# First scores ahead of the last Mish block, and an output product cut at the attention outputs

## The chip, the cores and the metric

The kernel runs on one core of a Trainium2 chip. That core has a matrix engine (TensorE, PE in the profile; PEld are its weight loads), a vector engine (VectorE, DVE), an activation engine (ScalarE, ACT), a general engine (GpSimd, POOL) and a queue that issues DMAs (SyncE, SP). The engines run side by side. Each works through its own list of instructions in order, and they meet only through semaphores. The metric is the device time in microseconds (us) of one launch; lower is better. Three runs of the kernel before took 481.72, 482.39 and 482.79 us.

## What is computed

Attention with a softmax whose denominator has one extra term, over 8 batches of 12 heads, 448 rows, head size 64. Its output, seen as 3584 rows of 768, goes through a layer of 2048 with the Mish function:

```python
scores = scale * np.matmul(q, k.transpose(0, 1, 3, 2))
m = np.max(scores, axis=-1, keepdims=True)
e = np.exp(scores - m)
attn = e / (np.sum(e, axis=-1, keepdims=True) + np.exp(-m) + 1e-09)
x = (attn @ v).transpose(0, 2, 1, 3).reshape(3584, 768)
h = x @ w_in
g = h * np.tanh(np.log1p(np.exp(h)))     # Mish
out = g @ w_out
```

## The kernel before

**Units.** Two heads make a pair, three pairs make a unit, and two units hold one batch. Unit u works on the scores and exponentials of its own three pairs, on the attention outputs of unit u-1, on half of the first layer (x @ w_in, eight blocks of 128 features) for batch (u-2)//2, and on parts of the output product (g @ w_out) of earlier batches. Units 2 to 15 have scores; units 4 to 15 are "grouped": the order of work in their twelve steps is written out by hand in the table `GROUPED` (L484). That table has one list for even and one for odd units. Units 16 to 19 finish the layer. The program has a manual schedule: instructions stand on each engine in the order in which the Python code emits them.

**Names used from here on.** All are of one grouped unit.

- S0, S1, S2, S4, ... are score steps of two matmuls (L247 and L250, 64 rows of the array each, side by side); R3, R7 and R11 are the fourth step of each pair, one full matmul (L255). Steps 0-3 belong to the first pair, 4-7 to the second, 8-11 to the third.
- r0 to r11 are the maxima of these steps on DVE (L269), e0 to e11 their exponentials on ACT (L282). A step S has two exponentials, a step R one. Step s of a pair uses PSUM tile sc0, sc1 or sc2; step R uses mo1.
- A0, A1, A2 are the attention outputs of the pairs of the unit before (eight matmuls, L354). They go to mo1 (in odd units the third goes to sc0) and X0, X1, X2 take them out on DVE (L363).
- A *fill* is two matmuls of the output product (L443); a *part* is eight fills for 128 rows and either a half (384) or a quarter (192) of the columns. A part takes its PSUM tile, mo0, with its first fill. DVE empties it after the last (evacuation E, L430), and only then can the next part begin: mo1 is kept out of the free list in grouped units.
- M0 to M7 are the blocks of the first layer (six matmuls, L377, then one Mish on ACT, L383). They use sc0, mo0, mo1, sc0, mo0, mo1, mo0, mo1 (`MISH_BANK`, L514). T1, T3 and T5, after M1, M3 and M5, turn q and k of the next unit on PE (L189); DVE takes out q (L208), ACT takes out k (L218).
- D0, D1, D2 are the DMAs that turn the exponentials for the attention output (L321, tile eT). They follow the denominators (L295, L299) and the normalisation (L317 on DVE for two pairs, L315 on POOL for the third), which need all exponentials of the unit. They sit in SP's queue with the loads of q, k, v (L128) and the stores (L408).

**Order of a unit.** Twelve steps: step n emits its exponentials e(n), flushes the evacuations that are due (`flush_late`), and then what the table lists: fills ("fill", count), scores ("sc", steps), an attention output ("av", pair). Behind the twelve steps come M0 to M7 with T1, T3, T5 and the normalisation between them, and after M7 the scores S0, S1, S2 of the next unit (L680). Last stands a small exponential (L689) that loads the exponential's table on ACT. The other switch of tables comes with the first Mish.

The table of even units before, with the three scores in front: `S0 S1 S2 | 6 fills, A0 | 2 fills, R3 S4 S5 | 4 fills | S6, A1 | 2 | 2, R7 S8 S9 | 4 | 4, S10, A2 | 3 | 2, R11 | 3 | M0...`. Odd units start with 5 and 3 fills ahead of `R3 S4 S5`, have A0 where even units have A1, A1 where those have A2, and A2 behind R11.

`plan` (L463) gives each unit its parts, 32 fills in all (24 in unit 4). The rows of the plan list (group, row block, first quarter, number of quarters).

Of the kernel before, what the change touches and what calls it, by code (L numbers as in the profile page):

```python
# [19 lines left out]
def kernel(  # L20
# [24 lines left out]
    FF_U = FF_T // UNITS_PER_B  # L45
    NH = d_model // 2
    SCALE = 1.0 / float(D) ** 0.5
    N_PAIRS = B * HP
    STEPS = 4
# [3 lines left out]
    def pool(name, bufs, space=None):  # L53
# [18 lines left out]
    sc_tiles = [  # L72
        psum.tile([128, 2, 512], FP32, tag=f"sc{i}", name=f"sc{i}") for i in range(3)
    ]
    mo_tiles = [psum.tile([128, 512], FP32, tag=f"mo{i}", name=f"mo{i}") for i in range(2)]
# [32 lines left out]
    def flush_late():  # L108
        while late:
            late.popleft()()  # L110
# [40 lines left out]
    def load_w(n):  # L151
        for _ in range(min(n, len(pieces))):
            dst, src = pieces.popleft()
            nc.gpsimd.dma_start(out=dst, in_=src.rearrange("(a p) c -> p a c", p=128))
# [301 lines left out]
    first_mm2 = 2 * UNITS_PER_B  # L456
# [6 lines left out]
    plan = {}  # L463
    for g in range(B // 2):
        u0 = first_mm2 + 4 * g
        if g == 0:
            plan[u0] = [(0, 0, 0, 2), (0, 1, 0, 2), (0, 2, 0, 1)]
            plan[u0 + 1] = [(0, 0, 2, 2), (0, 1, 2, 2), (0, 2, 1, 1), (0, 2, 2, 2)]
        else:
            plan[u0] = plan.pop(u0) + [(g, 0, 0, 2), (g, 1, 0, 1), (g, 0, 2, 2)]  # L470
            plan[u0 + 1] = [(g, 1, 2, 2), (g, 2, 0, 2), (g, 1, 1, 1), (g, 2, 2, 2)]
        plan[u0 + 2] = [(g, 4, 0, 2), (g, 4, 2, 2), (g, 5, 0, 1), (g, 5, 1, 2)]
        plan[u0 + 3] = [(g, 3, 0, 2), (g, 3, 2, 2), (g, 5, 3, 1), (g, 6, 0, 2)]
        if g < B // 2 - 1:
            plan[u0 + 4] = [(g, 6, 2, 2)]
        else:
            plan[u0 + 3] += [(g, 6, 2, 1), (g, 6, 3, 1)]
# [4 lines left out]


    GROUPED = (  # L484
        (
            [("fill", 6), ("av", 0)],
            [("fill", 2), ("sc", (3, 4, 5))],
            [("fill", 4)],
            [("sc", (6,)), ("av", 1)],
            [("fill", 2)],  # L490
            [("fill", 2), ("sc", (7, 8, 9))],
            [("fill", 4)],
            [("fill", 4), ("sc", (10,)), ("av", 2)],
            [("fill", 3)],
            [("fill", 2), ("sc", (11,))],
            [("fill", 3)],
            [],
        ),
        (
            [("fill", 5)],  # L500
            [("fill", 3), ("sc", (3, 4, 5))],
            [("fill", 4)],
            [("sc", (6,)), ("av", 0)],
            [("fill", 2)],
            [("fill", 2), ("sc", (7, 8, 9))],
            [("fill", 4)],
            [("fill", 4), ("sc", (10,)), ("av", 1)],
            [("fill", 3)],
            [("fill", 2), ("sc", (11,))],
            [("fill", 1), ("av0", 2)],  # L510
            [("fill", 2)],
        ),
    )
    MISH_BANK = (0, 1, 2, 0, 1, 2, 1, 2)  # L514
    to_gather = deque()

# [63 lines left out]
    for u in range(UNITS_PER_B, N_UNITS + 2 * UNITS_PER_B):  # L580
        attn = u < N_UNITS
        filler = deque()
        for part in plan.get(u, []):
            filler.extend(mm2_part(*part))
        total, done, acc = sum(w for _, w in filler), 0, 0.0
        p0 = u * UNIT_PAIRS
        grouped = attn and p0 >= GROUP_FROM
        if u == N_UNITS:
            mo_free.append(mo_tiles[1])
        end = min((u + 1) * UNIT_PAIRS, N_PAIRS) * STEPS  # L590

        for n in range(steps):
            pi, s = divmod(n, STEPS)
            p, idx = p0 + pi, p0 * STEPS + n
            late_tp = u == UNITS_PER_B and n == STEPS
            if late_tp:
                transpose_pair(p0 + 2)
            exps(idx)
            if grouped:
                flush_late()  # L600
                for what, arg in GROUPED[u % 2][n]:
                    if what == "fill":
                        for _ in range(min(arg, len(filler))):
                            fn, w = filler.popleft()
                            fn()
                            done += w
                    elif what in ("av", "av0"):
                        bank = mo_tiles[1] if what == "av" else sc_tiles[0][:, 0, :]
                        av_pair(p0 - UNIT_PAIRS + arg, bank=bank)
                    else:  # L610
                        flush_late()
                        for i in arg:
                            scores(p0 * STEPS + i)
                if n in LOAD_AT:
                    load_pair(p0 + LOAD_AT.index(n) + LEAD)
                    cast_pair(p0 + LOAD_AT.index(n) + LEAD - 1)
                if u - UNITS_PER_B < len(W_AT):
                    load_w(W_AT[u - UNITS_PER_B].get(n, 0))
                continue
            if late_tp:  # L620
                evac_qk(p0 + 2)
            if u == UNITS_PER_B + 1:
                for part in TURN_AT[1].get(n, []):
                    turn_on_pe(*part)
            flush_late()
            acc += weight[n]
            want = int(total * acc / sum(weight) + 1e-6)
            while done < want:
                fn, w = filler.popleft()
                fn()  # L630
                done += w
            scores_ahead(end)
            if n in LOAD_AT:
                load_pair(p0 + LOAD_AT.index(n) + LEAD)
                cast_pair(p0 + LOAD_AT.index(n) + LEAD - 1)
            if u - UNITS_PER_B < len(AV_AT):
                early = AV_AT[u - UNITS_PER_B]
                if n in early:
                    av_pair(early[n])
                if u == UNITS_PER_B:  # L640
                    for part in TURN_AT[0].get(n, []):
                        turn_on_pe(*part)
            elif u == N_UNITS and n in LAST_AV_AT:
                av_pair(p0 - UNIT_PAIRS + LAST_AV_AT.index(n))
            if u - UNITS_PER_B < len(W_AT):
                load_w(W_AT[u - UNITS_PER_B].get(n, 0))
        assert done == total

        moe = u < N_UNITS + UNITS_PER_B
        b, w = (u - UNITS_PER_B) // UNITS_PER_B, u % UNITS_PER_B  # L650
        nxt = p0 + UNIT_PAIRS
        todo = sorted(range(p0, nxt), key=lambda p: p in BY_PE)
        to_group = attn and nxt >= GROUP_FROM
        if to_group and nxt == GROUP_FROM:
            flush_late()
            mo_free.remove(mo_tiles[1])
            rg["next"] = N_PAIRS * STEPS
        for f in range(FF_U):
            if moe:
                bank = sc_tiles[0][:, 0, :] if f == 1 else None  # L660
                if to_group:
                    bank = (sc_tiles[0][:, 0, :], None, mo_tiles[1])[MISH_BANK[f]]
                mm1_mish(b, w * FF_U + f, bank)
                if f == 6 and to_gather:
                    gather_mid(to_gather.popleft())
            if u == UNITS_PER_B and f in (2, 6):
                load_w(1)
            if not attn:
                continue
            if f == 0:  # L670
                denominators(att[p0]["whole"])
                normalise(todo[0], dma=todo[0] not in BY_PE)
            if f in (1, 3, 5):
                transpose_pair(nxt + f // 2, bank=f // 2 % 2)
                evac_qk(nxt + f // 2)
            if not to_group and f in (4, 6):
                scores_ahead(nxt * STEPS + f // 2 - 1)
            if f == FF_U - 1 and not to_group:
                scores_ahead(nxt * STEPS + 3)
            if f == FF_U - 1 and to_group and nxt < N_PAIRS:  # L680
                for s in range(3):
                    scores(nxt * STEPS + s)
            if f == 3:
                normalise(todo[1], dma=todo[1] not in BY_PE)
            if f == 4:
                normalise(todo[2], dma=todo[2] not in BY_PE, on_pool=True)
        if attn and u + 1 < N_UNITS:

            nc.scalar.activation(out=one, in_=zero, func=AF.Exp)  # L689
        if moe and w == UNITS_PER_B - 1:  # L690
            to_gather.append(b)
            if u == N_UNITS + UNITS_PER_B - 1:
                gather_mid(to_gather.popleft())
# [32 lines left out]
```

## Time and profile before

| what | value |
|---|---|
| median of three runs | 482.39 us |
| the profiled execution, its own time | 483.19 us |
| its span, first to last instruction | 481.1 us |
| mean granted TensorE clock | 0.982 |
| PE busy | 439.6 us, 91% |
| ACT busy | 348.7 us, 72% |
| DVE busy | 328.9 us, 68% |
| POOL busy | 193.9 us, 40% |
| chain that ended last, by engine | PE 72%, DVE 14%, ACT 6%, issue 4%, DMA 3% |

The profiled execution takes 2.09 us more than its span: that is what lies around the first and the last instruction. "Busy" of PE counts the modelled end of each matmul and so overlaps a little; where a matmul starts is the safer thing to read. An entry such as `[0.74 <-DVE negm L269]` at the end of a row of the timeline says how long the engine was idle before that row and whose instruction ended last before it went on.

### The profile page before, as it was taken

The page shows a single profiled execution, that of the slowest core. Times are in us where ns is not written, and L with a number is a line of the kernel's source. Part 1 is how long each engine was busy: PE and PEld are TensorE (multiplying, and loading weights), DVE is VectorE, ACT ScalarE, POOL GpSimd, SP SyncE. Part 2 cuts the span into 40 slices and gives each one's busy share as a digit, 9 for nine tenths or more (in the row PEclk, how much of TensorE's full clock was granted, in tenths as well). Part 3 has the DMA queues.
Part 4 walks back from the last instruction along what each step waited for, and adds up shares of the span by engine and source line. Part 5 has one row for each costly group of instructions (what it writes and reads, how often), then busy time and mean ns, then how long its engine had stood idle before and what let it go on. Part 6 is the DMA issues. An engine that isn't in the chain of part 4 may idle for free.

```text
span 481.1 us, 8897 instructions
## 1 busy us (share of the span) xinstructions
PE 439.6 (91%) x3064; PEld 237.6 (49%) x3064; DVE 328.9 (68%) x652; ACT 348.7 (72%) x919; POOL 193.9 (40%) x365
## 2 busy tenths in 40 slices
PE   4565887998899899999999999999999999999997
PEld 2233544544455454545455554545454545556565
DVE  4888987878786868777785968587777868330021
ACT  5979678879796879788887979697977979302300
POOL 4877809255616244253636344343535340300000
PEclk9998698999999999999999999999999999999999
DMA  8999959999999989898999999898999594860213
GB/s 220 226 240 205 239 99 234 160 197 244 188 217 266 215 225 216 224 194 235 206 241 173 252 156 245 185 223 210 203 228 201 153 180 117 143 153 1 67 33 100
DMA packets 202381, 90.37 MB, mean 188 GB/s; under 512 B 159072, under 2 KB 198880, under 8 KB 202336
## 3 DMA queue, kind: packets, MB, share of 16 engines
q1 hardware_dynamic: 194848, 83.51, 80.0%
q0 software_dynamic: 7488, 6.29, 8.5%
q8 instruction: 24, 0.39, 0.3%
q14 instruction: 21, 0.17, 0.1%
HBM read 45.61 MB, written 11.01 MB: 118 GB/s over the span
## 4 chain that ended last, share of the span: by engine, by line
PE 72%; DVE 14%; ACT 6%; issue 4%; DMA 3%; POOL 0%; DVEq 0%; SPq 0%; ACTq 0%; POOLq 0%
PE mo L443 26%; PE mo L377 21%; DVE negm L269 9%; PE sc L377 7%; PE sc L247 5%; PE mo L354 5%; ACT en L282 4%; PE sc L189 3%; DMA eT<-en 2%; DVE o_sb L430 2%; PE mo L332 2%; PE mo L255 1%; DVE en L317 1%; PE sc L354 1%; DMA k_f<-in_k_dram 1%
## 5 line engine op out<-in xcount | busy, mean ns | idle before, releaser
L282 ACT ACTIVATE en<-sc,negm 128x448 bf16<-128x448 f32 x300 | 186.6, 645 | 12.8 <-DVE negm L269 8.9
L269 DVE TENSOR_REDUCE negm<-sc 128x2 f32<-128x896 f32 (+1 forms) x156 | 158.0, 1048 | 37.9 <-PE sc L250 30.7
L443 PE MATMUL mo<-w_out_sb,gT 128*128 128x384 bf16 (+1 forms) x912 | 138.6, 301 | 1.5
L377 PE MATMUL mo<-xT,w_in_sb 128*128 128x448 bf16 x594 | 122.4, 352 | 0.6 <-DVE xT L363 0.6
L443 PEld LDWEIGHTS <-gT 128*128 128x128 bf16 x912 | 81.0, 98 | 58.5 <-issue 23.2
L383 ACT ACTIVATE gT<-mo 128x448 bf16<-128x448 f32 x99 | 53.9, 545 | 72.7 <-PE mo L377 72.7
L377 PEld LDWEIGHTS <-w_in_sb 128*128 128x128 bf16 x768 | 72.8, 98 | 66.5 <-issue 5.3
L315 POOL TENSOR_SCALAR en<-en,rden 128x448 bf16<-128x448 bf16 x122 | 77.7, 654 | 58.1 <-DVE rden L307 54.2
L430 DVE COPY o_sb<-mo 128x384 f32<-128x384 f32 (+1 forms) x65 | 32.5, 500 | 48.8 <-PE mo L443 47.6
L171 POOL CAST q_bf<-q_f 112x512 bf16<-112x512 f32 x47 | 28.9, 614 | 91.7 <-DMA q_f<-in_q_dram 90.9
L282 ACT ACTIVATION_READ_ACCUMULATOR en<-sc,negm 128x1 f32 x300 | 65.1, 217 | 0.0
L247 PE MATMUL sc<-kT,qT 64*128 64x448 bf16 x144 | 48.3, 386 | 17.2 <-ACT en L282 11.3
L317 DVE TENSOR_SCALAR en<-en,rden 128x448 bf16<-128x448 bf16 x214 | 58.9, 345 | 0.5
L250 PE MATMUL sc<-kT,qT 64*128 64x448 bf16 x144 | 48.6, 389 | 0.0
L354 PE MATMUL mo<-eT,v_bf 112*64 112x448 bf16 x336 | 41.0, 368 | 2.4 <-DMA eT<-en 1.5
L377 PE MATMUL sc<-xT,w_in_sb 128*128 128x448 bf16 x174 | 37.6, 352 | 0.2
L208 DVE TENSOR_SCALAR qT<-sc 128x448 bf16<-128x448 bf16 x39 | 15.2, 389 | 27.6 <-PE sc L189 27.6
L158 POOL CAST v_bf<-v_f 112x512 bf16<-112x512 f32 x48 | 29.6, 616 | 10.6 <-DMA v_f<-in_v_dram 10.1
L213 POOL COPY qr<-qT 64x64 bf16<-64x64 bf16 x36 | 8.8, 245 | 56.3 <-DVE qT L208 56.2
L172 POOL CAST k_bf<-k_f 112x512 bf16<-112x512 f32 x47 | 28.9, 614 | 4.2 <-DMA k_f<-in_k_dram 3.5
L354 PEld LDWEIGHTS <-v_bf 112*64 112x64 bf16 x384 | 18.6, 111 | 21.7 <-issue 11.9
L363 DVE CAST xT<-mo 128x448 bf16<-128x448 f32 x39 | 24.0, 617 | 7.2 <-PE mo L354 7.2
(55 smaller groups left out, 387.4 us busy)
## 6 DMA issues: line engine op xcount, KB each, us to landing
q_f<-in_q_dram SPq DMA_DIRECT2D x48, 224.0 KB, 5.2
k_f<-in_k_dram SPq DMA_DIRECT2D x48, 224.0 KB, 5.4
v_f<-in_v_dram SPq DMA_DIRECT2D x48, 224.0 KB, 5.5
w_in_sb<-in_moe_w_in_dram POOLq DMA_DIRECT2D x12, 256.0 KB, 6.0
w_out_sb<-in_moe_w_out_dram POOLq DMA_DIRECT2D x8, 384.0 KB, 7.7
out_dram<-o_sb SPq DMA_DIRECT2D x7, 336.0 KB, 3.2
out_dram<-o_sb SPq DMA_DIRECT2D x8, 288.0 KB, 4.9
out_dram<-o_sb SPq DMA_DIRECT2D x8, 240.0 KB, 4.1
```

The lines of the kernel that those rows point to most:

```text
L158: nc.gpsimd.tensor_copy(out=casted[p][2], in_=loaded.pop(p)[2])
L247: nc.tensor.matmul(sc[:, 0, 0:S], lhsT=qT[0:64, qa : qa + 128], rhs=kA, start=True, stop=True)
L250: nc.tensor.matmul(sc[:, 1, 0:S], lhsT=qT[64:128, qb : qb + 128], rhs=kB, start=True, stop=True)
L269: nc.vector.tensor_reduce(out=negm, in_=sc[:, 0 : len(cols), 0:S], axis=AX.X, op=ALU.max, negate=True)
L282: nc.scalar.activation(out=st["en"][:, :, c, 0:SP_], in_=sc[:, bk, 0:S].rearrange("q (j c) -> q j c", j=NT), func=AF.Exp, bias=st["negm"][ ...
L315: nc.gpsimd.tensor_scalar(scalar2=1.0, op0=ALU.mult, op1=ALU.mult, **args)
L317: nc.vector.tensor_scalar(scalar2=None, op0=ALU.mult, **args)
L354: nc.tensor.matmul(av[h * 64 : (h + 1) * 64, 0:S], lhsT=v_bf[:, h, j * D : (j + 1) * D], rhs=e_h, start=(j == 0), stop=(j == NT - 1),)
L377: nc.tensor.matmul(h_ps[:, 0:S], lhsT=w_in_sb[:, dm, ff * 128 : (ff + 1) * 128], rhs=xT[b][:, dm, :], start=(dm == 0), stop=(dm == DM_T - 1),)
L383: nc.scalar.activation(out=gT[b][:, ff, :], in_=h_ps[:, 0:S], func=AF.Mish)
L430: nc.vector.tensor_copy(out=o_sb[:, cols], in_=st["o"][:, 0:n_cols])
L443: nc.tensor.matmul(st["o"][:, 0:n_cols], lhsT=src[:, ff, c0 : c0 + 128], rhs=w_out_sb[:, ff, cols], start=(ff == 0), stop=(ff == FF_T - 1),)
```

## The change

The change does four things. `GROUPED` becomes one list for even and odd units: `8 fills, A0 | 2 fills, R3 S4 S5 | 3 | 3, S6, A1 | 3 | R7 S8 S9 | 3 | 2, S10, A2 | 8 | R11 | | M0...`. The parts in `plan` are put in another order, so that in each full unit come three halves and then a quarter; the fill counts then let each half end where an attention output follows. Unit 5 alone (`LATE_AV`) keeps its attention outputs late, the third behind R11 and into sc1. The scores S0, S1, S2 of the next unit go from behind M7 to in front of M7. The copy of 64 rows of g for the mixed row block (`gather_mid`, L387) goes from M6 to M2.

```diff
--- before.py
+++ after.py
@@ -465,12 +465,12 @@
         u0 = first_mm2 + 4 * g
         if g == 0:
             plan[u0] = [(0, 0, 0, 2), (0, 1, 0, 2), (0, 2, 0, 1)]
-            plan[u0 + 1] = [(0, 0, 2, 2), (0, 1, 2, 2), (0, 2, 1, 1), (0, 2, 2, 2)]
+            plan[u0 + 1] = [(0, 0, 2, 2), (0, 1, 2, 2), (0, 2, 2, 2), (0, 2, 1, 1)]
         else:
-            plan[u0] = plan.pop(u0) + [(g, 0, 0, 2), (g, 1, 0, 1), (g, 0, 2, 2)]
-            plan[u0 + 1] = [(g, 1, 2, 2), (g, 2, 0, 2), (g, 1, 1, 1), (g, 2, 2, 2)]
-        plan[u0 + 2] = [(g, 4, 0, 2), (g, 4, 2, 2), (g, 5, 0, 1), (g, 5, 1, 2)]
-        plan[u0 + 3] = [(g, 3, 0, 2), (g, 3, 2, 2), (g, 5, 3, 1), (g, 6, 0, 2)]
+            plan[u0] = plan.pop(u0) + [(g, 0, 0, 2), (g, 0, 2, 2), (g, 1, 0, 1)]
+            plan[u0 + 1] = [(g, 1, 2, 2), (g, 2, 0, 2), (g, 2, 2, 2), (g, 1, 1, 1)]
+        plan[u0 + 2] = [(g, 4, 0, 2), (g, 4, 2, 2), (g, 5, 0, 2), (g, 5, 2, 1)]
+        plan[u0 + 3] = [(g, 3, 0, 2), (g, 3, 2, 2), (g, 6, 0, 2), (g, 5, 3, 1)]
         if g < B // 2 - 1:
             plan[u0 + 4] = [(g, 6, 2, 2)]
         else:
@@ -482,35 +482,34 @@
 
 
     GROUPED = (
-        (
-            [("fill", 6), ("av", 0)],
-            [("fill", 2), ("sc", (3, 4, 5))],
-            [("fill", 4)],
-            [("sc", (6,)), ("av", 1)],
-            [("fill", 2)],
-            [("fill", 2), ("sc", (7, 8, 9))],
-            [("fill", 4)],
-            [("fill", 4), ("sc", (10,)), ("av", 2)],
-            [("fill", 3)],
-            [("fill", 2), ("sc", (11,))],
-            [("fill", 3)],
-            [],
-        ),
-        (
-            [("fill", 5)],
-            [("fill", 3), ("sc", (3, 4, 5))],
-            [("fill", 4)],
-            [("sc", (6,)), ("av", 0)],
-            [("fill", 2)],
-            [("fill", 2), ("sc", (7, 8, 9))],
-            [("fill", 4)],
-            [("fill", 4), ("sc", (10,)), ("av", 1)],
-            [("fill", 3)],
-            [("fill", 2), ("sc", (11,))],
-            [("fill", 1), ("av0", 2)],
-            [("fill", 2)],
-        ),
+        [("fill", 8), ("av", 0)],
+        [("fill", 2), ("sc", (3, 4, 5))],
+        [("fill", 3)],
+        [("fill", 3), ("sc", (6,)), ("av", 1)],
+        [("fill", 3)],
+        [("sc", (7, 8, 9))],
+        [("fill", 3)],
+        [("fill", 2), ("sc", (10,)), ("av", 2)],
+        [("fill", 8)],
+        [("sc", (11,))],
+        [],
+        [],
     )
+    GROUPED_LATE_AV = (
+        [("fill", 8), ("sc", (3,))],
+        [("fill", 3), ("sc", (4, 5))],
+        [("fill", 2)],
+        [("fill", 3), ("sc", (6,)), ("av", 0)],
+        [("fill", 3)],
+        [("sc", (7, 8, 9))],
+        [("fill", 3)],
+        [("fill", 2), ("sc", (10,)), ("av", 1)],
+        [("fill", 8)],
+        [("sc", (11,))],
+        [("av1", 2)],
+        [],
+    )
+    LATE_AV = first_mm2 + 1
     MISH_BANK = (0, 1, 2, 0, 1, 2, 1, 2)
     to_gather = deque()
 
@@ -598,14 +597,14 @@
             exps(idx)
             if grouped:
                 flush_late()
-                for what, arg in GROUPED[u % 2][n]:
+                for what, arg in (GROUPED_LATE_AV if u == LATE_AV else GROUPED)[n]:
                     if what == "fill":
                         for _ in range(min(arg, len(filler))):
                             fn, w = filler.popleft()
                             fn()
                             done += w
-                    elif what in ("av", "av0"):
-                        bank = mo_tiles[1] if what == "av" else sc_tiles[0][:, 0, :]
+                    elif what in ("av", "av1"):
+                        bank = mo_tiles[1] if what == "av" else sc_tiles[1][:, 0, :]
                         av_pair(p0 - UNIT_PAIRS + arg, bank=bank)
                     else:
                         flush_late()
@@ -656,12 +655,15 @@
             mo_free.remove(mo_tiles[1])
             rg["next"] = N_PAIRS * STEPS
         for f in range(FF_U):
+            if f == FF_U - 1 and to_group and nxt < N_PAIRS:
+                for s in range(3):
+                    scores(nxt * STEPS + s)
             if moe:
                 bank = sc_tiles[0][:, 0, :] if f == 1 else None
                 if to_group:
                     bank = (sc_tiles[0][:, 0, :], None, mo_tiles[1])[MISH_BANK[f]]
                 mm1_mish(b, w * FF_U + f, bank)
-                if f == 6 and to_gather:
+                if f == 2 and to_gather:
                     gather_mid(to_gather.popleft())
             if u == UNITS_PER_B and f in (2, 6):
                 load_w(1)
@@ -677,9 +679,6 @@
                 scores_ahead(nxt * STEPS + f // 2 - 1)
             if f == FF_U - 1 and not to_group:
                 scores_ahead(nxt * STEPS + 3)
-            if f == FF_U - 1 and to_group and nxt < N_PAIRS:
-                for s in range(3):
-                    scores(nxt * STEPS + s)
             if f == 3:
                 normalise(todo[1], dma=todo[1] not in BY_PE)
             if f == 4:
```

## The prediction

> **What bounds it now.** First the page's chain that ended last: PE holds 72% of it. Then the stretches of the grouped units, even unit 8 above odd unit 9 (length, then busy time of PE, PEld, DVE, ACT, POOL):
>
> ```profile
> 208.48:234.40 25.92, 25.75 (x183) 13.59 (x183) 20.10 (x41) 21.87 (x58) 11.25 (x23) 1.00 0.99 217
> 234.40:261.15 26.75, 25.83 (x182) 13.59 (x181) 19.53 (x40) 21.77 (x58) 11.29 (x24) 1.00 0.95 211
> ```
>
> The same PE work takes 0.83 us more in the odd unit; the other pairs of units repeat this. PE sets the pace, but it waits somewhere in odd units. The timeline of PE in unit 9 has the place:
>
> ```profile
> 236.90 0.35 PE L255 MATMUL mo<-kT,qr 128*128 128x448 bf16 x1
> 237.19 0.36 PE L247 MATMUL sc<-kT,qT 64*128 64x448 bf16 x1
> ...
> 238.29 0.35 PE L247 MATMUL sc<-kT,qT 64*128 64x448 bf16 x1 [0.74 <-DVE negm L269]
> ```
>
> These are R3, S4, S5. The row names DVE's r3, but S5 needs sc1 free, and so the second half of e1. ACT's timeline shows that it ends at 238.24:
>
> ```profile
> 237.51 0.64 ACT L282 ACTIVATE en<-sc,negm 128x448 bf16<-128x448 f32 x1
> 238.03 0.21 ACT L282 ACTIVATION_READ_ACCUMULATOR en<-sc,negm 128x1 f32 x1
> ```
>
> In unit 8 S5 starts at 212.69 while r3 runs from 212.68 to 213.29, so r3 isn't what it waits for. Unit 8 has A0 (0.88 us) ahead of R3 and comes late enough. Its own waits are smaller, for PSUM to be emptied: fills after A2 start at 220.47, 0.2 late, because mo0 is still full:
>
> ```profile
> 219.38 0.95 PE L354 MATMUL mo<-eT,v_bf 112*64 112x448 bf16 x8
> 220.47 1.78 PE L443 MATMUL mo<-w_out_sb,gT 128*128 128x384 bf16 x10
> ```
>
> DVE, held by two maxima, empties mo0 only then (its timeline):
>
> ```profile
> 220.06 0.35 DVE L430 COPY o_sb<-mo 128x192 f32<-128x192 f32 x1
> ```
>
> Last, the DMAs D0-D2: a row of SP's timeline in unit 8, the time to landing (min, median, max, units 7 to 14) from the view of tile eT, and A0 of unit 6, the one attention output of grouped units that waited long for such a DMA:
>
> ```profile
> 226.59 13.38 SPq L321 DMA_TRANSPOSE eT<-en  x3
> ```
>
> ```profile
> DMA to landing us min/median/max: 6.1/6.1/7.8
> ```
>
> ```profile
> 157.80 0.95 PE L354 MATMUL mo<-eT,v_bf 112*64 112x448 bf16 x8 [1.51 <-DMA eT<-en]
> ```
>
> **Prices, by start-to-start distances.** A fill of a half 0.326 us (16 matmuls 2.61), of a quarter 0.165; S 0.19; R 0.19; A 0.78; M 1.134; T 0.39. Each change between whole-array matmuls and 64-row or 64-column ones costs 0.10 more (S to S 0.19, S to fill 0.28). A unit has 14 such changes before and after, so nothing is added or saved there. DVE: r 1.00 (R: 0.53), E 0.48 (quarter 0.27), X 0.53. ACT: e 0.61. Latencies: S start to r 0.41, A start to X 1.06, r end to e 0.04; a tile is free 0.06 after its reader's end. Times below count from the end of M7.
>
> **A common unit after.** On ACT, Mish M7, table, first exponential keep their distance: e0 at 2.16 (207.65 to 209.81), e1 ends 4.72. S0-S2 stand at -1.81, -1.61, -1.42, so r0-r2 are done by 1.69, not 3.59.
>
> PE: 8 fills to 2.61; A0 2.71 to 3.59, over which E (2.81 to 3.37) is hidden; 2 fills to 4.24; R3 waits for X0 (3.77 to 4.38) until 4.44; S4 4.72; S5 4.91, with sc1 free at 4.77: the stall of odd units is gone. Six fills from 5.19; S6 7.25; A1 7.54 to 8.42; three fills to 9.40. DVE by then: r3 4.83, r4 5.36, r5 6.36, E 7.36, r6 7.84, X1 8.84 to 9.45. R7 9.51 (0.11 of waiting), S8 9.79, S9 9.98; five fills 10.26 to 11.89; S10 11.99; A2 12.28 to 13.16; the quarter to 14.48. DVE: r8 10.43, r9 11.43, E 12.43 to 12.99, r10 12.91, X2 13.91 to 14.52. The evacuations of the halves end under A0, A1, A2. R11 waits 0.10 for X2, until 14.58, and all of M0 to M7 stands behind it; M0 at 14.77. (The half's E ahead of r10, where a quarter's was, makes r10 0.2 later; e10 waits 0.04 for it.)
>
> ACT: e4 6.48, e7 10.56, e8 11.55, e10 14.03, e11 15.63; Mish of M0 2.15 after e11 as in unit 8, so 17.78 to 18.32. M3 needs its tile at 18.56: 0.18 to spare. T3 at 19.70 needs q of T1 by 19.40. S1 and S2 need k and q of T5 out of sc1 and sc2: ACT's copy stands behind the Mish of M5, 23.0 to 23.5, S1 at 24.2. S0-S2 pass only M7 on PE; their maxima fall into 2.0 to 2.3 us of idle DVE. M6 ends at 23.88, S0-S2 and M7 take 1.90: **25.78 us a unit**. Before, the starts of S0 (207.74, 233.62, 260.41) give 25.88 even and 26.79 odd.
>
> The copy at M2 (0.42, once in two units) falls into 1.8 us of idle DVE before the q of T3; without this cover it would delay that by 0.3. D0 is issued 3.46 after e11 (19.09, the DVE steps before it unchanged), D1 and D2 follow at 4.3 each; loads behind them start at 6.2 of the next unit (6.5 and 6.7 before). Landings at 25.4, 29.7, 34 stand against A0, A1, A2 at 28.5, 33.3, 38.1: 3 to 4 us to spare. Number and sizes of DMAs don't change; the stores move within the unit and stay ahead of D0.
>
> **First grouped units.** The end of M7 of unit 3 comes 0.77 later (101.04 to 101.80), S0-S2 now being ahead of it. Unit 4 has only 24 fills and waits for exponentials: the same walk gives 26.17 with the 0.6 wait at T3 that it has now; M7 ends 127.97 (126.60). Unit 5 with late outputs gives M0 at 15.31, 26.32 in all. But A0 of unit 6 waits for a DMA already: the first D0 of unit 4 took 8.66 on SP beside the loads of w_out, the loads behind are late, D0 of unit 5 goes out at 148.61 and lands at 157.75. I take it up to 0.8 later, as unit 4's normalisation is: A0 at 158.1 (157.8 to 158.5). From A0 to the end of M7 is 23.07, so 181.17; before 180.86.
>
> **The sum.** Units 7 to 14: 181.17 + 8 x 25.78 = 387.41 (391.54 before). M0 of unit 15: +14.77 = 402.18; before 408.06. Gain 5.88. Lost again: e11 of unit 15 ends 2.2 later against M0 than now, so D2 goes out 14.3 after M0 (13.6 if D1 holds SP for the usual 4.3 instead of its 4.98) and lands 6.1 later, 19.7 to 20.4, where A2 of unit 16 stands at 19.75: 0 to 0.65, I take 0.5. At the very end, row block 5 is completed one half (2.6 us) before the end instead of 5.2, so two stores of 384 KB together stand ahead of the last small ones in SP's queue; bounds 0 (they land in 4.1, in time) and 0.6 (their share of a busy queue); I take 0.2, nearer to the landing row. Net 5.2: span 481.1 - 5.2 = 475.9, and from the median **477.2 us** (the profiled execution stands 0.8 above the median).
>
> ScalarE's table is the place where the Trainium skill speaks against this. Its page "ScalarE: Activation LUTs", section "What ACT_TABLE_LOAD costs", puts a switch at about 2.66 us with a drain. Here the load takes 1.28, and from the end of Mish (208.38) to the first exponential (209.81) it is 1.43. By the page's price, two switches in the chain would make M3 wait 2 x 1.23 - 0.18 = 2.3 us in nine units, an estimate of 498 us. The profile has 27 such loads, all of 1.28, and the row decides.
>
> **Rivals.**
>
> *ScalarE's chain takes over* (14%). M3 has 0.18 to spare. If e11 comes 0.5 later than walked, M3 waits 0.32 in nine units, 2.9 in all: 479-480, say 480.1. For: e11 hangs on R11, X2, r10 in a row, DVE being full from 9.9 to 14.4. Against: e11 stands at 15.48 and 15.23 in units 8 and 9 now, near my 15.63.
>
> *D0 too late, slower* (9%). A0 now stands 9.4 us behind D0's issue in odd units too, where it had 13.7 (226.59 to 240.29). If D0 lands later than 9.4, every unit waits. The slow landings of this trace, 9.1 and 11.4 (units 5 and 4), average 10.25; from 10.0 on nine units lose the 5.2. At 10.4 they lose 9 x 0.85 = 7.6: 484.8. Against: both had w_out's loads or their aftermath beside them; units 7 to 14 show 6.1 to 7.8.
>
> *Transfers set the pace* (7%). The 16 DMA engines show a share of 0.95 to 1.05 in most units. If two units can't go below the 52.67 of now, only the last attention phase gains: 5.2 - 4.4 = 0.8, 481.6. Against: unit 14 had a share of 0.82 and the same length; SP is idle 1.7 us before D0 in unit 8 and 1.5 in unit 9.
>
> *A table switch dearer than its row* (1%): M3 waits as long as the switches grow, less 0.18; from 0.6 more a unit on the gain is gone.
>
> **How the numbers follow.** The forecast has 69%, with 475.4 to 479.0 by 0.2 us a unit either way. The range goes down to 475.0 and up to 481.6, the case of the transfers; D0 too late and the dearer switch, 10%, stay outside. A measurement of this kernel tells 0.2% (1 us) from no change. Faster by that: 0.69 and most of the 14% = 0.81. Same: the transfers and a rest of the chain, 0.08. Slower: 0.11.
>
> **What would show it.** Odd and even units both near 25.8 from S0 to S0; no 0.7 us wait at S5; fills after A1 and A2 start without one; r0-r2 end before fills do; M3 right behind M2. Wrong it would be if M3 waits for the Mish of M0, if A0 waits for eT beyond unit 6, or if the loads' casts on POOL delay T3 or T5.

## The result and the profile after

The changed kernel takes 479.12 us (median of five runs, 477.58 to 479.47) against 482.63 us of the kernel before (481.72 to 484.34) on the same chip: a ratio of 0.9915, 95% interval 0.9888 to 0.9943. The profiled execution took 479.26 us with a span of 477.2, 3.9 less than the 481.1 before. Forecast were 477.2 us and a span of 475.9.

The same two units in the view by stretches, each from the end of one M7 to the next, unit 8 above unit 9 (length, then busy time of PE, PEld, DVE, ACT, POOL, granted clock, DMA share, GB/s):

```profile
207.97:233.89 25.92, 25.83 (x182) 13.46 (x181) 20.20 (x41) 21.61 (x57) 11.22 (x23) 1.00 1.01 214
233.89:259.68 25.79, 25.76 (x183) 13.48 (x182) 19.57 (x40) 21.61 (x57) 11.05 (x23) 1.00 0.96 222
```

The odd unit is 0.96 us shorter (26.75 before), the even one is as long as it was (25.92). PE's timeline of unit 9 shows the place where the wait stood: A0, two fills, R3, S4, S5, and on to the next fills.

```profile
236.59 0.95 PE L354 MATMUL mo<-eT,v_bf 112*64 112x448 bf16 x8
237.47 0.82 PE L443 MATMUL mo<-w_out_sb,gT 128*128 128x384 bf16 x4
238.32 0.35 PE L255 MATMUL mo<-kT,qr 128*128 128x448 bf16 x1
238.60 0.36 PE L247 MATMUL sc<-kT,qT 64*128 64x448 bf16 x1
238.80 0.35 PE L247 MATMUL sc<-kT,qT 64*128 64x448 bf16 x1
239.09 2.12 PE L443 MATMUL mo<-w_out_sb,gT 128*128 128x384 bf16 x12
```

S5 starts 0.20 behind S4, which is the price of a step and no wait. Fills behind A1 and A2 of units 8 and 9 no longer wait either. The starts of S0, unit by unit (read from PE's timeline, differences in us), carry the rest of this section:

| unit | 4 | 5 | 6 | 7 | 8 | 9 | 10 | 11 | 12 | 13 | 14 |
|---|---|---|---|---|---|---|---|---|---|---|---|
| before | 25.56 | 26.80 | 27.46 | 26.79 | 25.88 | 26.79 | 25.88 | 26.80 | 25.87 | 26.80 | 25.87 |
| after | 25.62 | 27.01 | 27.80 | 25.78 | 25.92 | 25.79 | 25.78 | 25.84 | 25.78 | 25.79 | 25.78 |

Units 7, 9, 11 and 13 give 1.0 us each. Units 5 and 6 give nothing, they take 0.55 more. PE's timeline of units 5 and 6 after shows what stands there:

```profile
129.92 0.81 PE L443 MATMUL mo<-w_out_sb,gT 128*128 128x384 bf16 x4 [0.43 <-DMA w_out_sb<-in_moe_w_out_dram]
131.45 1.14 PE L443 MATMUL mo<-w_out_sb,gT 128*128 128x384 bf16 x6 [0.53 <-DVE o_sb L430]
...
158.99 0.95 PE L354 MATMUL mo<-eT,v_bf 112*64 112x448 bf16 x8 [1.83 <-DMA eT<-en]
```

The first part of unit 5 waits for a load of w_out, for which the kernel before didn't wait, and A0 of unit 6 waits 1.83 us for its DMA, where it waited 1.51. SP's timeline shows the transfers that these waits belong to. D0 to D2 of unit 4 hold the queue for 18.9 us, where those of unit 8 before took 13.4, and what is queued behind them is late. Most of that is no news: in the kernel before they started at the same time and held it for 18.1. After:

```profile
120.98 18.92 SPq L321 DMA_TRANSPOSE eT<-en  x3
140.00 1.00 SPq L408 DMA_DIRECT2D out_dram<-o_sb  x2
...
148.95 15.39 SPq L321 DMA_TRANSPOSE eT<-en  x3
```

Before:

```profile
120.98 18.06 SPq L321 DMA_TRANSPOSE eT<-en  x3
...
148.61 15.30 SPq L321 DMA_TRANSPOSE eT<-en  x3
```

So D0 of unit 5 goes out 0.34 later than before. It then landed in 10.0 us instead of 9.1, which is the larger part.

The page's chain that ended last now has 8% DMA where it had 3%:

```profile
PE 70%; ACT 9%; DMA 8%; DVE 5%; POOL 3%; issue 2%; SPq 1%; DVEq 0%; ACTq 0%; POOLq 0%
```

### The profile page after: what moved, and what is told of

Same layout as the page of the kernel before. It is cut to its first block, busy times and chain, and to the rows that moved or that the text cites. A ratio compares the mean times of both kernels' runs of the same rounds, so it can differ in the third digit from the quotient of the medians.

```text
span 477.2 us, 8887 instructions
## 1 busy us (share of the span) xinstructions
PE 439.1 (92%) x3064; PEld 236.0 (49%) x3064; DVE 329.6 (69%) x652; ACT 346.6 (73%) x919; POOL 193.5 (41%) x365
## 4 chain that ended last, share of the span: by engine, by line
PE 70%; ACT 9%; DMA 8%; DVE 5%; POOL 3%; issue 2%; SPq 1%; DVEq 0%; ACTq 0%; POOLq 0%
PE mo L443 27%; PE mo L377 19%; ACT en L282 7%; PE mo L354 6%; PE sc L377 6%; PE sc L247 5%; DVE negm L269 3%; PE sc L189 3%; DMA w_out_sb<-in_moe_w_out_dram 2%; DMA v_f<-in_v_dram 2%; DMA eT<-en 2%; PE mo L255 2%; POOL en L315 1%; DMA w_in_sb<-in_moe_w_in_dram 1%; PE mo L189 1%
## 5 line engine op out<-in xcount | busy, mean ns | idle before, releaser
L377 PE MATMUL mo<-xT,w_in_sb 128*128 128x448 bf16 x594 | 124.4, 352 | 0.6 <-DMA w_in_sb<-in_moe_w_in_dram 0.6
L315 POOL TENSOR_SCALAR en<-en,rden 128x448 bf16<-128x448 bf16 x122 | 76.1, 641 | 55.7 <-DVE rden L307 52.8
L430 DVE COPY o_sb<-mo 128x192 f32<-128x192 f32 (+1 forms) x65 | 32.5, 499 | 56.6 <-PE mo L443 44.4
L282 ACT ACTIVATION_READ_ACCUMULATOR en<-sc,negm 128x1 f32 x300 | 62.2, 207 | 0.0
L317 DVE TENSOR_SCALAR en<-en,rden 128x448 bf16<-128x448 bf16 x214 | 60.5, 352 | 0.5
L247 PE MATMUL sc<-kT,qT 64*128 64x448 bf16 x144 | 47.1, 385 | 12.7 <-ACT en L282 11.2
L354 PE MATMUL mo<-eT,v_bf 112*64 112x448 bf16 x376 | 45.9, 367 | 3.0 <-DMA eT<-en 1.8
L250 PE MATMUL sc<-kT,qT 64*128 64x448 bf16 x144 | 47.4, 387 | 0.0
L363 DVE CAST xT<-mo 128x448 bf16<-128x448 f32 x44 | 27.0, 616 | 10.3 <-PE mo L354 9.6
L269 DVE TENSOR_REDUCE negm<-mo 128x1 f32<-128x448 f32 x36 | 22.3, 620 | 10.5 <-PE mo L255 10.5
L354 PEld LDWEIGHTS <-v_bf 112*64 112x64 bf16 x384 | 18.9, 111 | 21.6 <-issue 14.6
L282 ACT ACTIVATE en<-mo,negm 128x448 bf16<-128x448 f32 x36 | 23.1, 640 | 7.7 <-DVE negm L269 7.7
```

What stands on the lines that cost most here:

```text
L247: nc.tensor.matmul(sc[:, 0, 0:S], lhsT=qT[0:64, qa : qa + 128], rhs=kA, start=True, stop=True)
L250: nc.tensor.matmul(sc[:, 1, 0:S], lhsT=qT[64:128, qb : qb + 128], rhs=kB, start=True, stop=True)
L269: nc.vector.tensor_reduce(out=negm, in_=sc[:, 0 : len(cols), 0:S], axis=AX.X, op=ALU.max, negate=True)
L282: nc.scalar.activation(out=st["en"][:, :, c, 0:SP_], in_=sc[:, bk, 0:S].rearrange("q (j c) -> q j c", j=NT), func=AF.Exp, bias=st["negm"][ ...
L315: nc.gpsimd.tensor_scalar(scalar2=1.0, op0=ALU.mult, op1=ALU.mult, **args)
L317: nc.vector.tensor_scalar(scalar2=None, op0=ALU.mult, **args)
```

## The experiments

The theory: the gain comes from A0 at the head of odd units, which keeps PE busy until e1 has left sc1; the new parts only keep that at 25.8, and the earlier S0 to S2 add nothing; what the prediction missed is a backlog of transfers in units 4 to 6. Four kernels take the change apart, four test the backlog and the rest, and three were run side by side at the end. Ratios are to the kernel before, on the same chip.

### The scores alone

```diff
         for f in range(FF_U):
+            if f == FF_U - 1 and to_group and nxt < N_PAIRS:
+                for s in range(3):
+                    scores(nxt * STEPS + s)
             if moe:
...
-            if f == FF_U - 1 and to_group and nxt < N_PAIRS:
-                for s in range(3):
-                    scores(nxt * STEPS + s)
```

> The kernel before with one part of the change alone: S0 to S2 in front of M7; tables, parts and the copy at M6 as before. Theory (the gain comes from the new tables; the earlier scores only shift the exponentials against PE): S5 still waits for e1, which stays 4.77 us behind the end of M7, while that end comes 0.77 later behind M6. So odd units lengthen from 26.79 to 27.5, even ones from 25.88 to 26.3, and the time is 488 us (ratio 1.012). Rival (the earlier maxima are the gain): both parities at 26.0 or below, time 480 or less.

Measured: 489.7 us, ratio 1.0128 (1.0097 to 1.0159). Odd units take 27.57, even ones 26.39 or 26.40. PE's timeline of unit 9 in this kernel, M7 (the row at 234.29) and what follows:

```profile
234.29 1.31 PE L377 MATMUL mo<-xT,w_in_sb 128*128 128x448 bf16 x6
235.44 2.76 PE L443 MATMUL mo<-w_out_sb,gT 128*128 128x384 bf16 x16
238.04 0.35 PE L255 MATMUL mo<-kT,qr 128*128 128x448 bf16 x1
238.98 0.35 PE L247 MATMUL sc<-kT,qT 64*128 64x448 bf16 x1 [0.59 <-ACT en L282]
...
240.21 0.35 PE L247 MATMUL sc<-kT,qT 64*128 64x448 bf16 x1 [0.86 <-ACT en L282]
```

S4 waits for e0 and S5 for e1: with S0 to S2 out of the way, PE reaches them sooner after M7, while the exponentials start when they always did, 2.16 us behind M7, because the Mish of M7 and the table come first on ACT. The rows now name ACT as the releaser. ACT's timeline has the end of e1 at 240.15, 0.06 ahead of S5, while r3 on DVE had ended at 239.39:

```profile
239.94 0.21 ACT L282 ACTIVATION_READ_ACCUMULATOR en<-sc,negm 128x1 f32 x1
```

The row of the kernel before named DVE, whose r3 happened to end 0.02 us later than e1; this run settles that it was e1. Alone, this part of the change costs 6 us.

### The tables and parts alone

The changed kernel with those three lines put back behind M7; nothing else differs from it.

> The changed kernel with S0 to S2 put back behind M7. Theory: PE has the same work and the same small waits, odd and even units both at 25.8, the time within 0.7 us of the changed kernel's 479.1. Rival (the earlier scores are needed for it): a wait of 0.3 us or more at R3, S5 or M3 in every unit, units at 26.1 or above, time 481.5 or more.

Measured: 478.72 us, ratio 0.9900 (0.9876 to 0.9924). Units 7 to 14 take 25.78 or 25.79, unit 8 25.92, as in the changed kernel. With the new tables the place of S0 to S2 has no weight: what they cost PE ahead of M7 they don't cost behind it, and no wait depends on it.

### The even list for all

```diff
-                for what, arg in GROUPED[u % 2][n]:
+                for what, arg in GROUPED[u % 2 if u == first_mm2 + 1 else 0][n]:
```

> The kernel before with one edit: every grouped unit but unit 5 uses the list of the even units, so A0 stands at the head of odd units too; nothing else changes. Theory (the odd units' wait at S5 is what the change removes): odd units 25.9 like even ones, no 0.7 us wait at S5, time 478.3 (ratio 0.991). Rival (the halves ending at attention outputs and the earlier scores carry the gain): 481 or more.

Measured: 478.00 us, ratio 0.9892 (0.9860 to 0.9923). Units 7 to 14 take 25.87 or 25.88. This edit of the kernel before gives as much as the whole change. Of the 1.0 us that an odd unit gains, 0.92 comes with the even list, whose A0 at the head keeps PE busy until sc1 is free, and 0.09 with the new list and parts. (The even list also moves A1, A2 and some fills; no run moves A0 by itself.) In this profile D0 of unit 5 landed in 8.3 us and A0 of unit 6 didn't wait.

### The old order of the parts

The lines of `plan` as before, the rest as changed: the third part is the quarter again.

> The changed kernel with the old order of the parts (half, half, quarter, half). Theory: the quarter is now the third part, its first fills are too short to cover X1, so R7 waits 0.6 instead of 0.1, and the last half must wait 0.5 behind A2 for the quarter's evacuation, which stands behind r9; a unit takes 26.6 us and the time is 486 (ratio 1.008). Rival (the order is of no weight, since the work is the same): 25.8 a unit and 479.

Measured: 488.19 us, ratio 1.0096 (1.0063 to 1.0130), units 26.73. PE's timeline in a unit of this kernel has the two waits where the theory put them, R7 behind X1 and the last half behind the quarter's evacuation:

```profile
246.22 0.35 PE L255 MATMUL mo<-kT,qr 128*128 128x448 bf16 x1 [0.40 <-DVE xT L363]
...
249.54 0.65 PE L443 MATMUL mo<-w_out_sb,gT 128*128 128x384 bf16 x3 [0.38 <-DVE o_sb L430]
```

The idle times in the rows go by modelled ends. Counted from start to start with the prediction's prices, R7 waits 0.58 (0.09 after) and the last half 0.45 (none after); the difference, 0.94, is the 0.95 that a unit is longer. So the order of the parts isn't cosmetic: the fill counts of the new list need the halves first. The list of the even units before ran the old order at 25.87; that it can because it has other fill counts at these places is argued, not tested.

### Weight loads earlier

```diff
-    W_AT = ({5: 1, 9: 1}, {1: 1, 4: 1, 5: 1, 7: 1, 9: 1, 11: 1}, {3: 1, 5: 1, 7: 1, 9: 1})
+    W_AT = ({5: 1, 9: 1}, {1: 1, 4: 1, 5: 1, 7: 1, 9: 1, 11: 1})
...
             if u == UNITS_PER_B and f in (2, 6):
-                load_w(1)
+                load_w(5 if f == 2 else 1)
```

> The changed kernel with the last four weight loads moved forward: five pieces instead of one at M2 of unit 2, none in unit 4. In both kernels the DMA engines' share is 0.17 between 64 and 70 us and 1.2 to 1.3 from 118 to 136. Theory (what the prediction missed is the backlog of transfers that the last loads of w_out leave in units 4 to 6): the wait of 0.43 for w_out in unit 5 and that of 1.83 for eT at A0 of unit 6 go, D0 of unit 4 lands in under 9 us instead of 12.3; S0 of unit 7 near 178.1 instead of 180.37; time 476.8. Rival (the transfers are bound by their sum, wherever the loads stand): the waits move to unit 3 or 4 and the time stays at 479.

Measured: 478.07 us, ratio 0.9891 (0.9870 to 0.9912). D0 of unit 4 landed in 6.7 us; the view by source line of its DMA, after above this kernel:

```profile
DMA to landing us min/median/max: 12.3/12.3/12.3
```

```profile
DMA to landing us min/median/max: 6.7/6.7/6.7
```

Both waits are gone: units 5 and 6 take 26.43 and 25.78, together 2.60 less than after. The wait for w_out proves little by this, since it stands in the first profile of the changed kernel alone: in the repeated one, and in those of the tables alone and of the copy at M6, unit 5 takes 26.43 without it. The wait at A0 of unit 6 stands in seven of the nine profiles with the loads as they were (0.50 to 1.97 us) and in none of the four with the loads moved forward. D0 of unit 4 landed in 9.8 to 12.3 us in those nine and in 6.0 to 6.8 in these four.

The time fell by less than that, and S0 of unit 7 stands at 180.19, not near 178.1: in the profiled execution unit 4 took 27.27 instead of 25.62. The last section has the reason, TensorE's clock, and not the loads. The run with the highest mean granted clock of the six, 0.985, took 476.69, near the 476.8 expected; the five others, at 0.974 to 0.981, took 477.80 to 479.00.

### Weight loads earlier, scores behind M7, unit 5 on the common list

This is the kernel of the tables alone with the edit above, and with `GROUPED` in unit 5 too.

> As w_early, with S0 to S2 behind M7 again and unit 5 on the common list. Theory: unit 5 falls from 26.4 to 25.8, since D2 of unit 4 now lands ahead of A2, and the place of S0 to S2 is of no weight: 476.3, 0.987 of the kernel before. Rival (unit 5 needs its late outputs for the transfers all the same): A2 of unit 5 waits over 1 us, 477.5 or more.

Measured: 476.71 us, ratio 0.9862 (0.9839 to 0.9885). S0 of unit 7 stands at 178.90. Unit 5 takes 26.16, 0.27 less than on its late list instead of the 0.6 expected; A2 doesn't wait there.

### Unit 5 on the common list, the loads as they are

> The changed kernel with unit 5 on the common list, the loads as they are. Theory: A2 of unit 5 comes about 2 us ahead of the landing of D2 and waits, but A0 of unit 6 waits for its own DMA anyway and takes that up; S0 of unit 7 within 0.6 of 180.4, time 479. Rival (the wait at A2 adds to the one at A0): S0 of unit 7 at 182, time 481.

Measured: 478.92 us, ratio 0.9918 (0.9890 to 0.9945). S0 of unit 7 stands at 180.28. The wait came at A1, 1.02 us, not at A2, and A0 of unit 6 waited 0.50 instead of 1.83: as expected, the queue of transfers sets the end of unit 6, and what PE waits ahead of it costs nothing. The late list of unit 5 brings nothing that can be measured.

### The copy back at M6

> The changed kernel with the copy of the mixed row block back at M6. Theory: DVE idles at either place; units 25.8, 479. Rival: the copy at M6 delays the maxima r0 to r2 that now fall there, and units 8, 10, 12, 14 lengthen by 0.2 or more.

Measured once: 478.76 us, units 25.78 or 25.79 (unit 8 25.91). The copy is of no weight at either place.

### Three side by side

First the changed kernel once more.

> The changed kernel unchanged, beside the next two on one chip. Theory and rival both: 479, ratio 0.9915 of the kernel before.

Measured: 479.29 us, ratio 0.9899 (0.9866 to 0.9932).

> The kernel of w_early_tables once more. Theory (its gain over the changed kernel is the transfers' wait and unit 5, 2.2 to 2.6 us): ratio 0.986, interval below that of the changed kernel. Rival (the difference was a matter of the chip or the run): within 1 us of the changed kernel.

Measured: 477.27 us, ratio 0.9865 (0.9824 to 0.9905). The medians differ by 2.0 us, a little less than expected, and the intervals overlap here. In the profiles units 5 and 6 take 51.85 together against 56.01, but some 1.6 of that difference is the clock of the last section; the first profile of the changed kernel has 54.81.

The third is the kernel before with two edits, `GROUPED[0][n]` in every grouped unit and the earlier weight loads.

> The kernel before with the list of the even units in all grouped units, unit 5 too, and the four weight loads moved forward; scores, parts and copy as before. Theory (odd list and loads are all there is to gain, the rest of the change is worth 0.09 us a unit): units 25.9 throughout, no wait for w_out or for eT at A0, time 477.3, within 1 us of best_again. Rival (the new parts are needed once the transfers are out of the way): 478.5 or more.

Measured: 476.39 us, ratio 0.9835 (0.9798 to 0.9873), units 25.87 or 25.88 from 5 to 14. This kernel and the one above it can't be told apart. Both are faster than the kernel before; that this one is faster than the changed kernel too rests on medians 2.9 us apart, with intervals that still touch; of its six runs five are below all six of the changed kernel (478.38 and more), the sixth took 478.39. It has neither the earlier scores nor the new parts nor the late list.

## Why the prediction was right, and where it was off

**The stall of odd units.** Read from the row of S5 and from e1's end, put down to sc1, and removed by A0 at the head: right. The even list alone shows that this is nearly all of the gain, and the scores alone that the releaser was e1. The rest of the change, which the prediction walked through as one design, turned out not to be needed.

**The length of a unit.** Walked to 25.78, measured at 25.78 or 25.79 in most units. Small waits stood where the walk had them: in unit 8 R3, R7 and R11 each start 0.06 behind the end of X0, X1 and X2. The spare time of M3 was to be 0.18. ACT's timeline of unit 8 after has the Mish of M0, PE's has M3:

```profile
225.88 0.54 ACT L383 ACTIVATE gT<-sc 128x448 bf16<-128x448 f32 x1
```

```profile
226.65 1.30 PE L377 MATMUL sc<-xT,w_in_sb 128*128 128x448 bf16 x6
```

The Mish ends at 226.42, the tile is free 0.06 later, and M3 starts at 226.65: 0.17 to spare. ScalarE's chain did not take over, except in unit 15, where M3 waited 0.22 (PE is through with M2 at 407.14, M3 starts at 407.36, 0.06 behind the Mish of M0). The walk had 0.18 to spare there too, but no T stands between the blocks of that unit, and T1's 0.39 less ahead of M3 turns the 0.18 into a wait of 0.21.

**The first grouped units.** This is the term of the sum that was mis-sized. The end of M7 of unit 6 was put at 181.17 and came at 182.19, 1.0 later. Unit 4 took 25.62 instead of 26.17, since the 0.6 wait at T3 shrank to 0.05. Unit 5 took 27.01 instead of 26.32: 0.43 of it is the wait for w_out, which the prediction did not price, though it said that the loads of w_out lie beside D0. A0 of unit 6 came at 158.99, outside the bounds of 157.8 to 158.5: D0 of unit 5 was issued at 148.95, within what was expected, but landed in 10.0 us, not 9.1. The prediction took the landing time over from the kernel before, and that is what it had too small. In the nine profiles with the loads as they were this DMA landed in 8.3 to 10.5 us, in the four with the loads moved forward in 7.9 to 8.1, and there A0 doesn't wait; so the cause is shown to be the transfers. In part the miss belongs to this execution: in the five other profiles with the new list and the loads as they were, A0 of unit 6 came at 158.07 to 158.68.

**The sum from there.** Units 7 to 14 took 206.46 (206.24 forecast), the last attention phase 15.08 instead of 14.77, because X0 of unit 15 came 0.35 late (its row on DVE names an exponential as the releaser; why it should wait for one, no run shows). So M0 of unit 15 came 4.3 us earlier than before instead of 5.9. Between M0 of unit 15 and M0 of unit 16 0.33 was lost again, near the 0.5 forecast but not for its reason: D2 went out 13.45 behind M0 and landed at 423.29, 0.5 ahead of A2 (423.81), and nothing waited for it. M3's 0.22 is most of the loss; for the other 0.11 no row shows a wait. At the stores less than 0.1 was lost (0.2 forecast). Net 3.9 instead of 5.2.

**The rivals.** D0 to D2 landed in 6.1 to 8.2 us in units 7 to 14, well under the 10 from which this would have turned the sign; only unit 6 saw that mechanism. (The loss of 0.85 a unit that the prediction gives for a landing of 10.4 belongs to one of 10.25; at 10.4 it would be 1.0.) Transfers did not set the pace of the steady units: these shortened by 1.0 a pair at a DMA share of 0.96 to 1.01. The table switch kept its 1.28 us load, and 1.43 us from the end of the last Mish to the first exponential (234.63 to 236.06 in unit 9).

## What to carry to other kernels

When one parity of a loop is slower at equal work, look for the first row of the bound engine that waits, and check the named releaser against the other parity, where the same step didn't wait; the instruction that really frees the buffer may end within hundredths of the named one. Moving work out of a place where it covered someone else's latency makes that latency visible, so a reordering should be tried part by part: here one part alone cost 6 us and another gave all of the gain. And a gain in the steady loop is paid out only from where the start-up's transfers let go, so read the first iterations' queue as closely as the steady one.

## What the runs showed of the hardware

A wait of PE of about 2 us can cost almost as much again through its clock. In two of the profiles the granted clock fell within 1.1 us after such a wait: with the weight loads earlier (w_early) behind R11 of unit 4, which had waited 1.91 us, and in the repeated changed kernel behind A0 of unit 6, which had waited 1.97. The view by stretches, first six us each and then the slow stretch by itself, of the first and then of the second (the clock is the third number from the end):

```profile
116.00:122.00 6.00, 5.12 (x25) 2.46 (x25) 4.59 (x14) 5.32 (x14) 2.20 (x5) 0.72 0.76 153
122.00:128.00 6.00, 6.00 (x46) 3.33 (x46) 2.80 (x11) 3.25 (x7) 2.44 (x7) 1.00 0.90 169
117.62:121.03 3.41, 3.41 (x11) 1.39 (x10) 2.44 (x9) 2.92 (x7) 1.73 (x3) 0.50 0.79 160
```

```profile
154.00:160.00 6.00, 4.03 (x27) 2.21 (x26) 2.44 (x4) 5.71 (x15) 4.27 (x9) 0.97 1.24 192
160.00:166.00 6.00, 6.00 (x33) 2.26 (x31) 4.27 (x6) 3.30 (x10) 0.00 (x0) 0.75 1.08 208
159.61:163.02 3.41, 3.41 (x13) 1.09 (x12) 2.50 (x4) 1.08 (x5) 0.00 (x0) 0.50 1.10 226
```

In both the clock stood at half for 3.41 us, in which 1.7 us of full-speed work is lost. Unit 4 of the first took 1.65 us more than after; unit 6 of the second took 1.78 more, of which 0.14 is the longer wait. The start-up shows it in all thirteen profiles: PE waits 2.16 or 2.17 us once between 75 and 81 us (smaller waits stand beside it), and within 2.4 us the clock goes to half for 3.41 or 6.83 us.

The Trainium skill's page "TensorE: Matmul & The Clock Gate" (Part 1) describes a clock that is either full or half and is judged in free-running windows of 3.4 us; the length of the slow stretch here agrees with that. Its table in "Why this matters for your kernels" asks for no gaps over about 3 us; here gaps of 1.9 to 2.0 us were enough twice, while the same wait of 1.91 at R11 in the changed kernel's first profile, and 1.92 in others, left the clock at 1.00.

Windows whose place against the gap varies from run to run can't be the whole reason. The slow stretches begin and end at whole multiples of 3.41 us from one another (in w_early at 80.07, 86.90, 117.62 and 121.03). Counted on from 83.23, where one ends in the changed kernel's first profile, its wait at R11 (114.19 to 116.10) lies inside one such window, 113.94 to 117.36, just as that of w_early (114.97 to 116.88) lies inside 114.21 to 117.62. One kept its clock and the other didn't. What else decides, no run here shows.
